# A layer with local attention and a gated unit on one core: loads and copies of the first tiles re-ordered, the last tile cut into 512 and 128 columns

## The chip, the cores and the metric

The kernel runs on one core of one Trainium2 chip. A core has five engines that run side by side, each with its own stream of instructions in program order: TensorE (PE, matrix products into PSUM; its weight loads are listed apart as PEld), VectorE (DVE), ScalarE (ACT), GpSimd (POOL) and SyncE (SP, which mainly issues DMAs). ScalarE and GpSimd can issue DMAs too; "ACTq", "POOLq" and "SPq" are the queues on which an engine issues. The metric is the device time of one execution in microseconds.

## What is computed

One layer on 2048 tokens of 640 features, in bfloat16. The input is normalised without learned weights; from it a dilated local attention and a gated unit are computed, and both are added to the input:

```python
x = A_x                                   # [1, 2048, 640]
xn = (x - mean) / sqrt(var + 1e-5)
q, k, v = split(xn @ wqkv)                # 32 heads of 20 features
idx = pos[:, None] - 2 * arange(8)        # 8 keys: this token and every second one before it
logits = einsum("bhsd,bhswd->bhsw", q, k[idx]) * 20 ** -0.5   # idx < 0: -1e9
o = einsum("bhsw,bhswd->bhsd", softmax(logits), v[idx]) @ wo
h = (xn @ w_gate) * (xn @ w_up)           # 640 -> 1536
out = x + o + h @ w_down
```

## The kernel before, in words

The 2048 tokens are 16 tiles of 128; four tiles make a chunk of 512. For each tile the input is loaded (`load_x`), VectorE computes statistics in two halves of 320 columns (`st_in`, line 251) and their aggregate (`aggr_in`, lines 257 and 259), GpSimd raises the variance to the power -0.5 (line 265), and VectorE normalises in place (`apply_in`, line 270). The normalised tile is then transposed into `xnT`. For tiles 0 to 3 TensorE does this with five transposing matmuls (line 345) in two pieces of three and two, which are copied out of PSUM piece by piece (line 351); later tiles are transposed by DMA on SP (line 339).

From `xnT` come, chunk by chunk, queries and keys with 512 columns per matmul (`qk`, lines 407 and 414), values with 320 columns (`vproj`, lines 440 and 446), and the gated unit (`glu`, lines 614, 619 and 630: gate and up products on TensorE, both copied out by ScalarE, multiplied into `hT` by VectorE). Values go out to a DRAM buffer and come back as eight shifted copies (`load_v8`). The attention of a chunk (`prodlog`, `softmax`, `av`) is VectorE's: eight products q*k (line 478, tile `pw`) whose sums over the features of a head TensorE forms in two groups of 20 matmuls (line 488, tile `pl`; one group for four of the products). ScalarE copies the logits out (line 501), SP transposes them by DMA (line 509), and then follow the softmax and the weighted sum of the values, whose result `o` SP transposes into `oT` (line 597). At the end of a chunk, `down` forms for each tile two halves of 320 output columns: 12 matmuls over `hT` and `wd` (line 652) and five over `oT` and `wo` (line 655) each; VectorE adds the residual while it takes the result out of PSUM (line 661), and a DMA stores the tile (line 683; the last two tiles are stored from SP, the others from GpSimd).

The order on each engine is made by a planner when the program is built. Every piece of work is a `Step` with an engine, a cost, the time `occ` for which it holds its engine, and dependencies. `Plan.order` simulates all engines with these numbers and emits the steps in the order of their simulated starts; of the steps that are ready it takes the one with the least time to spare to the end. So the `cost` and `floor` numbers in the code move instructions about but are no times of the chip. `load(at, fn)` makes a DMA on SP, each behind the one before it, whose data the planner counts as landed not before `at`. `inline` chains the steps of the first tiles on VectorE in the written order. `hold(wq)` is a memset of two elements of `wq`: the load of `wq` writes the same tile and so waits for it, and the place of the memset on VectorE sets when SP can issue that load. The input tiles share five buffers, so x5 waits for the last reader of x0 (the transposes of tile 0), x6 for that of x1, and so on. Results in PSUM share six banks; `pe_main` chains the matmul steps on TensorE.

In the written order of the first tiles, SP issues x0 to x3, `wq` (behind the memset, which stands after the statistics of x0), x4, `wk`, x5, x6, x7; ScalarE issues the two halves of `wv`, then loads its activation table (line 177), and issues x8 later. TensorE first multiplies zeros (line 242), then follow the transposes of tile 0, the first half of its values, the transposes of tile 1, and so on. The first piece of tile 0's transposes is copied out by ScalarE and the second by VectorE; of the other tiles ScalarE copies both.

Of the kernel before, what the change touches and what calls it, by code (L numbers as in the profile page):

```python
# [9 lines left out]
ACT = mybir.ActivationFunctionType  # L10
ALU = mybir.AluOpType
# [20 lines left out]
class Plan:  # L32
# [8 lines left out]
    def add(self, eng, cost, fn, deps=(), occ=None, after=(), kb=0):  # L41
        s = Step(eng, cost, fn, deps, occ, after)
        s.kb = kb
        s.idx = len(self.steps)
        self.steps.append(s)
        return s
# [51 lines left out]
def kernel(  # L98
# [11 lines left out]
    nc = tc.nc  # L110
    P = nc.NUM_PARTITIONS
    x_flat = A_x.flatten_outer_dims()
    out_flat = out.flatten_outer_dims()
    S, D = x_flat.shape
# [8 lines left out]
    KT = D // P  # L123
    FT = F // P
    NT = S // P
# [4 lines left out]
    NS = D // 2  # L130
# [23 lines left out]
    add = plan.add  # L154
    T = {}
# [7 lines left out]
    def load_x(t, eng=None):  # L163
        def fn():
            x = new(("x", t), [P, D], BF, "x", 5)
            (eng or nc.sync).dma_start(out=x[:], in_=x_flat[t * P : (t + 1) * P, :])
        return fn
# [3 lines left out]
    def wload(dst, src, eng=None):  # L171
        return lambda: (eng or nc.sync).dma_start(out=dst[:], in_=src.rearrange("(i p) f -> p i f", p=P))
# [9 lines left out]
    def load(at, fn, deps=()):  # L182
        s = chain[0] = add("SP", 2.0, fn, deps, occ=0.45, after=[chain[0]])
        s.floor = at
        return s
# [5 lines left out]
    def hold(dst):  # L191
        return lambda: nc.vector.memset(dst[0:1, 0, 0:2], 0.0)
# [1 line left out]
    X[0] = load(3.0, load_x(0))  # L194
    X[1] = load(3.8, load_x(1))
    X[2] = load(4.9, load_x(2))
    X[3] = load(5.3, load_x(3))

    def consts0():
        wz = new("wz", [P, CS], BF, "gs", 3)  # L200
# [32 lines left out]
    C0 = add("POOL", 0.6, consts0)  # L233
    WV = [add("ACT", 4.6, part(0), [C0], occ=0.45)]
    WV.append(add("ACT", 5.6, part(1), occ=0.45, after=[WV[0]]))
    TB = add("ACT", 1.6, table, after=[WV[1]])
    CZ = add("POOL", 3.0, consts_z, [C0], occ=1.2)

    def warm():
# [28 lines left out]
    def ln_apply(t, lo=0, hi=D):  # L268
        def fn():
            nc.vector.tensor_scalar(T["x", t][:, lo:hi], T["x", t][:, lo:hi], scalar1=T["mv", t][:, 0:1],  # L270
                                    scalar2=T["rstd", t][:], op0=ALU.subtract, op1=ALU.mult)
        return fn
# [11 lines left out]
    def inline(eng, cost, fn, deps=(), occ=None):  # L284
        s = line[eng] = add(eng, cost, fn, deps, occ=occ, after=[line.get(eng)])
        return s

    def st_in(t, g, d=None):
        return inline("DVE", 0.48, ln_stats(t, g), [d or X[t]], 0.395)
# [5 lines left out]
    def apply_in(t):  # L295
        XT[t] = inline("DVE", 0.443, ln_apply(t), [RS[t]], 0.4)
# [12 lines left out]
    def pe_main(cost, fn, deps=(), banks=1):  # L309
        nonlocal main  # L310
        waits = []
        for k in range(banks):
            if len(ring) + k >= 6:
                waits.append(ring[len(ring) + k - 6])
        main = add("PE", cost + 0.165, fn, [main, *waits, *deps], occ=cost)
        return main
# [4 lines left out]
    def transposes(t):  # L321
        c, q = divmod(t, CH)

        def slot():
            if q == 0:
                new(("xnT", c), [P, KT, CS], BF, "xnT", 2)

        def pe():
            ps = new(("pst", t), [P, KT, P], BF, "ps", 6, psum)
            for g in range(KT):  # L330
                nc.tensor.transpose(ps[:, g, :], T["x", t][:, g * P : (g + 1) * P], ident[:])

        def ev():
            slot()
            nc.scalar.copy(T["xnT", c][:, :, q * P : (q + 1) * P], T["pst", t][:])

        def dma():
            slot()
            nc.sync.dma_start_transpose(out=T["xnT", c][:, :, q * P : (q + 1) * P], in_=T["x", t][:])

        def half(g0, g1, n):
            def pe():
                ps = new(("pst", t, n), [P, KT, P], BF, "ps", 6, psum)
                for g in range(g0, g1):
                    nc.tensor.transpose(ps[:, g, :], T["x", t][:, g * P : (g + 1) * P], ident[:])  # L345

            def ev():
                if n == 0:
                    slot()
                o, i = T["xnT", c][:, g0:g1, q * P : (q + 1) * P], T["pst", t, n][:, g0:g1, :]  # L350
                nc.scalar.copy(o, i) if t or n == 0 else nc.vector.tensor_copy(o, i)  # L351
            return pe, ev

        if t < CH:
            pa, ea = half(0, 3, 0)
            pb, eb = half(3, KT, 1)
            a = pe_main(0.17, pa, [XT.get((t, 0), XT[t])])
            TX[t] = add("ACT", 0.5, ea, [a], occ=0.42)
            ring.append(TX[t])
            a = pe_main(0.11, pb, [XT[t]])  # L360
            if t:
                TT[t] = add("ACT", 0.42, eb, [a, TX[t]], occ=0.33)
                behind(VE[t - 1][0], TT[t])
            else:
                TT[t] = inline("DVE", 0.4, eb, [a], 0.33)
            ring.append(TT[t])
        elif t < XDMA:
            a = pe_main(0.28, pe, [XT[t]])
            TT[t] = add("ACT", 0.695, ev, [a], occ=0.6)
            ring.append(TT[t])  # L370
        else:
            if c == 1:
                a = TT[t] = chain[0] = add("SP", 3.0, dma, [XT[t]], occ=1.28, after=[chain[0]])
            else:
                a = TT[t] = add("SP", 2.8, dma, [XT[t], GP.get(c - 2)], occ=1.28, kb=200)
        if t + 5 < W:
            X[t + 5] = load(11.9 + 0.45 * t, load_x(t + 5), [a])
        elif t == 3:
            X[t + 5] = add("ACT", 6.0, load_x(t + 5, nc.scalar), [a], occ=0.45)
        elif 8 <= t < NT - 5:  # L380
            X[t + 5] = add("POOL", 6.0, load_x(t + 5, nc.gpsimd), [a], occ=0.45, kb=160)
# [260 lines left out]
    def down(t):  # L642
        c, q = divmod(t, CH)
        load_xr(t)
        evs = []
        def pe(n, f0, f1, wo_part):
            if f0 == 0:
                new(("psD", t, n), [P, 512], F32, "ps", 6, psum)
            ps = T["psD", t, n]
            sl = slice(n * NS, (n + 1) * NS)  # L650
            for f in range(f0, f1):
                nc.tensor.matmul(ps[:, 0:NS], lhsT=T["hT", c, f][:, q * P : (q + 1) * P], rhs=wd[:, f, sl],  # L652
                                 start=(f == 0), stop=(f == FT - 1 and not wo_part))
            for g in range(KT if wo_part else 0):
                nc.tensor.matmul(ps[:, 0:NS], lhsT=T["oT", t][:, g, :], rhs=wo[:, g, sl],  # L655
                                 start=False, stop=(g == KT - 1 and f1 == FT))

        def evict(n, a):
            def ev():
                sl = slice(n * NS, (n + 1) * NS)  # L660
                nc.vector.tensor_tensor(T["xr", t][:, sl], T["psD", t, n][:, 0:NS], T["xr", t][:, sl], ALU.add)  # L661
            e = add("DVE", 0.486, ev, [a, XR[t]], occ=0.4)
            ring.append(e)
            evs.append(e)

        hs = [HT[c, f] for f in range(FT)]
        W2 = [OE[t], WL["d"], WL["o"]]
        if q == 0:
            cut = FT - 2
            for n in range(2):  # L670
                pe_main((cut + KT) * 0.136, lambda n=n: pe(n, 0, cut, True), [*hs[:cut], *W2], banks=n + 1)
            ends = [pe_main(2 * 0.136, lambda n=n: pe(n, cut, FT, False), hs[cut:], banks=0) for n in range(2)]
            for n in range(2):
                evict(n, ends[n])
            a = ends[1]
        else:
            for n in range(2):
                a = pe_main((FT + KT) * 0.136, lambda n=n: pe(n, 0, FT, True), [*hs, *W2])
                evict(n, a)
        DT[t] = a  # L680

        def st():
            (nc.sync if t >= NT - 2 else nc.gpsimd).dma_start(out=out_flat[t * P : (t + 1) * P, :], in_=T["xr", t][:])  # L683

        OB[t] = add("SP" if t >= NT - 2 else "POOL", 2.3, st, evs, occ=0.5)


    a = st_in(0, 0)
    a = st_in(0, 1, a)
    HQ = inline("DVE", 0.08, hold(wq))  # L690
    aggr_in(0, a)
    WQ = load(8.8, wload(wq, A_wqkv[:, 0:D]), [HQ])
    X[4] = load(9.2, load_x(4))
    WK = load(11.4, wload(wk, A_wqkv[:, D : 2 * D]))
    a = st_in(1, 0)
    a = st_in(1, 1, a)
    XT[0, 0] = inline("DVE", 0.31, ln_apply(0, 0, 3 * P), [RS[0]], 0.25)
    XT[0, 1] = inline("DVE", 0.26, ln_apply(0, 3 * P, D), [RS[0]], 0.2)
    XT[0] = XT[0, 1]
# [2 lines left out]
    transposes(0)  # L702
    vproj(0, (0,))
    a = st_in(2, 0)
    apply_in(1)
    transposes(1)
    a = st_in(2, 1, a)
    aggr_in(2, a)
    vproj(0, (1,))
    vproj(1, (0,))  # L710
# [90 lines left out]
```

## Time and profile before

| | us |
|---|---|
| median of 3 runs (266.08 to 266.64) | 266.16 |
| the profiled execution | 266.25 |
| its span in the trace | 264.5 |
| TensorE busy | 258.5 |
| VectorE busy | 215.5 |
| ScalarE busy | 106.5 |
| GpSimd busy | 40.7 |

All times of the profile are from one execution and count from the start of its span; the execution itself is 1.75 us longer than the span. A row gives the start, the length, the engine, the source line, the operation, and the tile written and the tile read; "x5" means that five instructions are put together, and in square brackets stands how long the engine had been idle and what ended that. A matmul's row is longer than its share of TensorE's time, since matmuls overlap: of the matmuls with 512 columns each row has 0.379 us, but 48 of them take 10.52 us in the chain of waits. For DMA issues, the time is that on the issuing engine, and "us to landing" counts from there.

### The profile page before, as it was taken

Reading aid. Unit: us, or ns where it says so; the run is one execution under the profiler, and the core shown is the slowest. Engines: PE = TensorE matmul, PEld = TensorE weight load, DVE = VectorE, ACT = ScalarE, POOL = GpSimd, SP = SyncE. Lnnn points to the kernel's source line nnn. Section 1 sums busy time; section 2 is a strip of 40 time slices with the busy share of each in tenths; the row PEclk is TensorE's granted clock in tenths of the full one; section 3 lists DMA queues with packets and bytes.
Section 4 is the critical chain, followed back from the end, with each engine's and each line's share of the span. In section 5 each row is a group of like instructions: output and inputs, shape, how many; then the busy total and the mean of one; then the engine's idle time right before and its main releaser. Section 6 shows DMA issues by size and latency. Waiting matters only on the chain.

```text
span 264.5 us, 4077 instructions
## 1 busy us (share of the span) xinstructions
PE 258.5 (98%) x1556; PEld 140.8 (53%) x1574; DVE 215.5 (81%) x338; ACT 106.5 (40%) x196; POOL 40.7 (15%) x84
## 2 busy tenths in 40 slices
PE   7999999999999999999999999999999999999994
PEld 2645445444676546444466754644447764445773
DVE  5785998999999999999994799999938999951221
ACT  2655556655300166555510135555552005554000
POOL 4541027000021221400001000410000104000000
PEclk9999999999999999999999999999999999999999
DMA  7968996999994194983142767891109467110001
GB/s 222 372 131 244 401 341 173 369 289 255 351 239 108 35 318 146 264 290 90 25 99 72 243 223 126 235 312 25 22 15 304 151 185 214 25 25 0 27 25 50
DMA packets 50563, 46.55 MB, mean 176 GB/s; under 512 B 24642, under 2 KB 47696, under 8 KB 50544
## 3 DMA queue, kind: packets, MB, share of 16 engines
q1 hardware_dynamic: 46704, 37.26, 49.7%
q0 software_dynamic: 2384, 8.05, 8.7%
q10 hardware_dynamic: 1456, 0.98, 1.2%
q8 instruction: 12, 0.20, 0.3%
q14 instruction: 7, 0.06, 0.1%
HBM read 35.39 MB, written 5.26 MB: 154 GB/s over the span
## 4 chain that ended last, share of the span: by engine, by line
PE 97%; DVE 1%; issue 0%
PE ps L614 39%; PE ps L652 20%; PE ps L407 16%; PE ps L655 8%; PE ps L440 7%; PE pl L488 4%; PE ps L242 2%; DVE st L251 1%; PE ps L345 1%; DVE x L270 0%; DVE xr L661 0%; DVE xnT L351 0%; DVE gs L201 0%; DVE mv L257 0%; DVE ve L259 0%
## 5 line engine op out<-in xcount | busy, mean ns | idle before, releaser
L614 PE MATMUL ps<-xnT,wg 128*128 128x512 bf16 x227 | 59.0, 379 | 0.7
L614 PE MATMUL ps<-xnT,wu 128*128 128x512 bf16 x240 | 59.6, 379 | 0.0
L652 PE MATMUL ps<-wd,hT 128*128 128x320 bf16 x384 | 57.4, 299 | 0.0
L478 DVE TENSOR_TENSOR pw<-q,k 128x2560 bf16<-128x2560 bf16 x32 | 46.4, 1484 | 3.2 <-ACT k L414 2.4
L652 PEld LDWEIGHTS <-hT 128*128 128x128 bf16 x384 | 37.3, 98 | 16.3 <-issue 1.3
L575 DVE TENSOR_TENSOR v<-v,a 128x5120 bf16<-128x5120 bf16 x16 | 45.1, 2818 | 0.0
L619 ACT CAST gs<-ps 128x512 bf16<-128x512 f32 x48 | 28.1, 586 | 37.6 <-PE ps L614 37.6
L614 PEld LDWEIGHTS <-wu 128*128 128x128 bf16 x240 | 23.5, 98 | 28.3
L614 PEld LDWEIGHTS <-wg 128*128 128x128 bf16 x240 | 23.3, 98 | 28.1 <-issue 0.8
L619 ACT CAST us<-ps 128x512 bf16<-128x512 f32 x48 | 28.1, 586 | 23.3 <-PE ps L614 23.3
L661 DVE TENSOR_TENSOR xr<-ps,xr 128x320 bf16<-128x320 f32 x32 | 14.9, 484 | 19.0 <-PE ps L655 15.7
L630 DVE TENSOR_TENSOR hT<-gs,us 128x512 bf16<-128x512 bf16 x48 | 19.6, 419 | 12.6 <-ACT us L619 12.5
L683 POOL DMA_DIRECT2D out_dram<-xr x14 | 7.6, 545 | 129.2 <-DVE xr L661 129.2
L655 PE MATMUL ps<-wo,oT 128*128 128x320 bf16 x160 | 27.0, 299 | 0.0
L584 DVE TENSOR_TENSOR v<-v 128x2560 bf16<-128x2560 bf16 x16 | 23.8, 1485 | 0.1
L440 PE MATMUL ps<-wv,xnT 128*128 128x320 bf16 x160 | 23.2, 299 | 0.4 <-ACT xnT L351 0.4
L407 PE MATMUL ps<-xnT,wk 128*128 128x512 bf16 x99 | 22.4, 379 | 0.1
L407 PE MATMUL ps<-xnT,wq 128*128 128x512 bf16 x96 | 22.0, 379 | 0.2
L440 PEld LDWEIGHTS <-xnT 128*128 128x128 bf16 x160 | 15.3, 98 | 7.5 <-ACT xnT L351 0.6
L655 PEld LDWEIGHTS <-oT 128*128 128x128 bf16 x160 | 15.7, 98 | 6.1
L501 ACT CAST L<-pl 128x512 bf16<-128x512 f32 x8 | 4.7, 586 | 34.2 <-PE pl L488 32.0
L414 ACT CAST q<-ps 128x512 bf16<-128x512 f32 x20 | 11.7, 586 | 13.0 <-PE ps L407 13.0
(55 smaller groups left out, 188.9 us busy)
## 6 DMA issues: line engine op xcount, KB each, us to landing
v<-vD SPq DMA_DIRECT2D x16, 1280.0 KB, 7.5
vD<-v_t POOLq DMA_DIRECT2D x16, 160.0 KB, 3.1
xr<-in_A_x_dram POOLq DMA_DIRECT2D x16, 160.0 KB, 6.0
out_dram<-xr POOLq DMA_DIRECT2D x14, 160.0 KB, 2.2
x<-in_A_x_dram SPq DMA_DIRECT2D x12, 160.0 KB, 5.8
wg<-in_B_w_gate_dram SPq DMA_DIRECT2D x1, 1920.0 KB, 7.8
wu<-in_B_w_up_dram SPq DMA_DIRECT2D x1, 1920.0 KB, 12.0
wd<-in_B_w_down_dram SPq DMA_DIRECT2D x1, 1920.0 KB, 15.0
```

The lines of the kernel that those rows point to most:

```text
L407: nc.tensor.matmul(T[key][:, 0:n], lhsT=(wk if r else wq)[:, i, j * P : (j + 1) * P], rhs=T["xnT", c][:, i, lo : lo + n], start=(i == 0), ...
L414: nc.scalar.copy(dst, T[key][:, 0:n])
L440: nc.tensor.matmul(T["psv", t, n][:, 0:NS], lhsT=T["xnT", c][:, i, q * P : (q + 1) * P], rhs=wv[:, i, n * NS : (n + 1) * NS], start=(i == ...
L478: nc.vector.tensor_tensor(p[:], T["q", c][:], T["k", c][:, :, DIL * i : DIL * i + CS], ALU.mult)
L575: nc.vector.tensor_tensor(v[:].rearrange("p w (j h) -> p w j h", j=Dh, h=H), v[:].rearrange("p w (j h) -> p w j h", j=Dh, h=H), T["a", n][ ...
L584: nc.vector.tensor_tensor(v[:, 0:4, :], v[:, 0:4, :], v[:, 4:8, :], ALU.add)
L614: nc.tensor.matmul(ps[:], lhsT=(wu if r else wg)[:, i, f * P : (f + 1) * P], rhs=T["xnT", c][:, i, :], start=(i == 0), stop=(i == KT - 1))
L619: nc.scalar.copy(s[:], T[key][:])
L630: nc.vector.tensor_tensor(h[:], T["gs", c, f][:], T["us", c, f][:], ALU.mult)
L652: nc.tensor.matmul(ps[:, 0:NS], lhsT=T["hT", c, f][:, q * P : (q + 1) * P], rhs=wd[:, f, sl], start=(f == 0), stop=(f == FT - 1 and not wo ...
L655: nc.tensor.matmul(ps[:, 0:NS], lhsT=T["oT", t][:, g, :], rhs=wo[:, g, sl], start=False, stop=(g == KT - 1 and f1 == FT))
L661: nc.vector.tensor_tensor(T["xr", t][:, sl], T["psD", t, n][:, 0:NS], T["xr", t][:, sl], ALU.add)
```

## The change

The diff has five parts.

1. x3 is loaded on ScalarE's queue behind the two halves of `wv`, in place of SP's.
2. The memset on which the load of `wq` waits stands behind the statistics of x1 (before: behind those of x0). In the written order `wk` follows after x4, x5 and x6.
3. ScalarE copies both pieces of tile 0's transposes.
4. The statistics of x2 are both written ahead of the normalisation of tile 1, and the planner's landing times for wq, x4 to x7 and wk are other numbers.
5. The last tile's output is computed as 512 and 128 columns in place of two times 320, and each piece is stored by its own DMA.

```diff
-    X[3] = load(5.3, load_x(3))
...
+    X[3] = add("ACT", 5.0, load_x(3, nc.scalar), occ=0.45, after=[WV[1]])
-    TB = add("ACT", 1.6, table, after=[WV[1]])
+    TB = add("ACT", 1.6, table, after=[X[3]])
...
-                nc.scalar.copy(o, i) if t or n == 0 else nc.vector.tensor_copy(o, i)
+                nc.scalar.copy(o, i)
...
+            TT[t] = add("ACT", 0.42, eb, [a, TX[t]], occ=0.33)
             if t:
-                TT[t] = add("ACT", 0.42, eb, [a, TX[t]], occ=0.33)
                 behind(VE[t - 1][0], TT[t])
-            else:
-                TT[t] = inline("DVE", 0.4, eb, [a], 0.33)
...
-            X[t + 5] = load(11.9 + 0.45 * t, load_x(t + 5), [a])
+            X[t + 5] = load((11.0, 11.5, 14.2)[t], load_x(t + 5), [a])
...
+        last = t == NT - 1
+        at = [0, 512, D] if last else [0, NS, D]
...
-            sl = slice(n * NS, (n + 1) * NS)
+            sl = slice(at[n], at[n + 1])
+            ps = T["psD", t, n][:, 0 : at[n + 1] - at[n]]
...
+        if last:
+            for n in range(2):
+                add("SP", 2.1, lambda n=n: st(at[n], at[n + 1]), [evs[n]], occ=0.5)
+        else:
+            OB[t] = add("SP" if t >= NT - 2 else "POOL", 2.3, st, evs, occ=0.5)
...
     a = st_in(0, 1, a)
-    HQ = inline("DVE", 0.08, hold(wq))
     aggr_in(0, a)
-    WQ = load(8.8, wload(wq, A_wqkv[:, 0:D]), [HQ])
-    X[4] = load(9.2, load_x(4))
-    WK = load(11.4, wload(wk, A_wqkv[:, D : 2 * D]))
     a = st_in(1, 0)
     a = st_in(1, 1, a)
+    HQ = inline("DVE", 0.08, hold(wq))
+    WQ = load(10.1, wload(wq, A_wqkv[:, 0:D]), [HQ])
+    X[4] = load(10.6, load_x(4))
...
     a = st_in(2, 0)
+    a = st_in(2, 1, a)
     apply_in(1)
     transposes(1)
-    a = st_in(2, 1, a)
+    WK = load(13.6, wload(wk, A_wqkv[:, D : 2 * D]))
     aggr_in(2, a)
```

In the built program the planner's order differs in one further stretch. In chunk 1, VectorE does the fourth product q*k right behind the third, before the softmax of chunk 0; TensorE does the first group of chunk 1's logits behind the third group of chunk 0's gated unit; ScalarE's copy of these logits and SP's transposing DMA move along with it.

More of the change, by code (lines that the diff above doesn't have):

```diff
@@ L648, in pe @@
                 new(("psD", t, n), [P, 512], F32, "ps", 6, psum)
-            ps = T["psD", t, n]
-            sl = slice(n * NS, (n + 1) * NS)
+            sl = slice(at[n], at[n + 1])
+            ps = T["psD", t, n][:, 0 : at[n + 1] - at[n]]
             for f in range(f0, f1):
-                nc.tensor.matmul(ps[:, 0:NS], lhsT=T["hT", c, f][:, q * P : (q + 1) * P], rhs=wd[:, f, sl],
+                nc.tensor.matmul(ps, lhsT=T["hT", c, f][:, q * P : (q + 1) * P], rhs=wd[:, f, sl],
                                  start=(f == 0), stop=(f == FT - 1 and not wo_part))
             for g in range(KT if wo_part else 0):
-                nc.tensor.matmul(ps[:, 0:NS], lhsT=T["oT", t][:, g, :], rhs=wo[:, g, sl],
+                nc.tensor.matmul(ps, lhsT=T["oT", t][:, g, :], rhs=wo[:, g, sl],
                                  start=False, stop=(g == KT - 1 and f1 == FT))
@@ L659, in ev @@
             def ev():
-                sl = slice(n * NS, (n + 1) * NS)
-                nc.vector.tensor_tensor(T["xr", t][:, sl], T["psD", t, n][:, 0:NS], T["xr", t][:, sl], ALU.add)
-            e = add("DVE", 0.486, ev, [a, XR[t]], occ=0.4)
+                w = at[n + 1] - at[n]
+                sl = slice(at[n], at[n + 1])
+                nc.vector.tensor_tensor(T["xr", t][:, sl], T["psD", t, n][:, 0:w], T["xr", t][:, sl], ALU.add)
+            cost = 0.153 + (at[n + 1] - at[n]) / 960
+            e = add("DVE", cost, ev, [a, XR[t]], occ=cost - 0.08)
             ring.append(e)
@@ L677, in down, with st @@
             for n in range(2):
-                a = pe_main((FT + KT) * 0.136, lambda n=n: pe(n, 0, FT, True), [*hs, *W2])
+                a = pe_main((FT + KT) * ((at[n + 1] - at[n]) / 2400 + 0.003), lambda n=n: pe(n, 0, FT, True), [*hs, *W2])
                 evict(n, a)
         DT[t] = a
-        def st():
-            (nc.sync if t >= NT - 2 else nc.gpsimd).dma_start(out=out_flat[t * P : (t + 1) * P, :], in_=T["xr", t][:])
-        OB[t] = add("SP" if t >= NT - 2 else "POOL", 2.3, st, evs, occ=0.5)
+        def st(lo=0, hi=D):
+            e = nc.sync if t >= NT - 2 else nc.gpsimd
+            e.dma_start(out=out_flat[t * P : (t + 1) * P, lo:hi], in_=T["xr", t][:, lo:hi])
+        if last:
[3 more added lines that the diff above has]
+            OB[t] = add("SP" if t >= NT - 2 else "POOL", 2.3, st, evs, occ=0.5)
     a = st_in(0, 0)
     a = st_in(0, 1, a)
-    HQ = inline("DVE", 0.08, hold(wq))
     aggr_in(0, a)
-    WQ = load(8.8, wload(wq, A_wqkv[:, 0:D]), [HQ])
-    X[4] = load(9.2, load_x(4))
-    WK = load(11.4, wload(wk, A_wqkv[:, D : 2 * D]))
     a = st_in(1, 0)
     a = st_in(1, 1, a)
+    HQ = inline("DVE", 0.08, hold(wq))
+    WQ = load(10.1, wload(wq, A_wqkv[:, 0:D]), [HQ])
+    X[4] = load(10.6, load_x(4))
     XT[0, 0] = inline("DVE", 0.31, ln_apply(0, 0, 3 * P), [RS[0]], 0.25)
```

## The prediction

> **What bounds the kernel now.** First the page: TensorE is busy for 98% of the span, its granted clock reads 9 in all 40 slices, and 97% of the chain that ended last lies on it.
> ```profile
> span 264.5 us, 4077 instructions
> PE 258.5 (98%) x1556; PEld 140.8 (53%) x1574; DVE 215.5 (81%) x338; ACT 106.5 (40%) x196; POOL 40.7 (15%) x84
> ...
> PE 97%; DVE 1%; issue 0%
> ```
> Then the busy time by stretch. From 12.12 us on TensorE lacks under 1 us in 245; before that it waits. So time can come only from the head (until the first query matmul at 12.12), from the tail after the last matmul, and from the few stalls between.
> ```profile
> 5.70:12.12 6.42, 6.01 (x52) 4.01 (x52) 5.28 (x19) 3.90 (x11) 3.19 (x7) 1.00 1.07 376
> 12.12:257.00 244.88, 243.93 (x1469) 132.60 (x1485) 206.40 (x304) 101.13 (x184) 34.95 (x68) 1.00 0.60 174
> ```
> The last two columns are the DMA share and GB/s: in the head all 16 DMA engines are full (1.07). Third, the timeline of the head. The reader is to see VectorE's copy of tile 0 (6.44) ahead of the statistics of x2 (6.65) and the normalisation of tile 1 (7.05), and TensorE's waits for VectorE at 7.53 and 9.51.
> ```profile
> 4.17 0.39 SPq L172 DMA_DIRECT2D wq<-in_A_wqkv_dram  x1
> ...
> 6.44 0.29 DVE L351 COPY xnT<-ps 128x256 bf16<-128x256 bf16 x1 [0.25 <-PE ps L345]
> 6.65 0.48 DVE L251 BATCH_NORM_STATS2 st<-x 128x6 f32<-128x320 bf16 x1
> ...
> 7.05 0.43 DVE L270 TENSOR_SCALAR x<-x,mv,rstd 128x640 bf16<-128x640 bf16 x1
> ...
> 7.53 0.28 PEld L345 LDWEIGHTS <-x 128*128 128x128 bf16 x5 [0.26 <-DVE x L270]
> ...
> 7.93 1.53 PE L440 MATMUL ps<-wv,xnT 128*128 128x320 bf16 x10
> ...
> 9.02 0.43 DVE L270 TENSOR_SCALAR x<-x,mv,rstd 128x640 bf16<-128x640 bf16 x1
> ...
> 9.51 0.28 PEld L345 LDWEIGHTS <-x 128*128 128x128 bf16 x5 [0.38 <-DVE x L270]
> ```
> Fourth, the DMA view one issue at a time, last column us from issue to landing: x2 (issued 1.74), the second half of wv (1.76), x3 (2.21), wq (4.17), wk (5.18). They land at 6.44, 7.86, 7.2, 10.2 and 12.9.
> ```profile
> x<-in_A_x_dram SPq DMA_DIRECT2D x1, 160.0 KB, 4.7
> ...
> wv<-in_A_wqkv_dram ACTq DMA_DIRECT2D x1, 400.0 KB, 6.1
> ...
> x<-in_A_x_dram SPq DMA_DIRECT2D x1, 160.0 KB, 5.0
> ...
> wq<-in_A_wqkv_dram SPq DMA_DIRECT2D x1, 800.0 KB, 6.0
> ...
> wk<-in_A_wqkv_dram SPq DMA_DIRECT2D x1, 800.0 KB, 7.7
> ```
> Last, two places further on: the logits of chunk 1, and the end.
> ```profile
> 79.30 1.48 DVE L478 TENSOR_TENSOR pw<-q,k 128x2560 bf16<-128x2560 bf16 x1
> ...
> 80.63 1.45 PE L488 MATMUL pl<-pw,Ek 128*32 128x512 bf16 x20
> ```
> ```profile
> 260.33 0.84 PE L655 MATMUL ps<-wo,oT 128*128 128x320 bf16 x5
> 261.21 0.49 DVE L661 TENSOR_TENSOR xr<-ps,xr 128x320 bf16<-128x320 f32 x1 [1.82 <-PE ps L655]
> ```
> The fourth matmul of the logits needs the product that ends at 80.78, after the group has begun; other such groups of 20 take 1.19 in the chain, this one 1.38.
>
> **The change, part by part.**
> *Tile 0's copies.* The 0.29 us copy leaves VectorE; ScalarE does it in 0.38 (its 128x256 row) behind its first copy (6.23 to 6.71), so until about 7.0. The fourth matmul of the values, which needs it, stands at 6.76 + 3 x 0.136 = 7.17: free, with 0.1 us of cover. On VectorE the statistics of x2 could now start at 6.1, after the 0.15 us operation at 6.04. But x2 lands at 6.44. So I put them at 6.46 and 6.86, and the normalisation of tile 1 behind both (it stood between them) at 7.26, 0.21 later than 7.05. Transposes of tile 1 then start at 7.74, five of them take 0.28 (a chain row), ten matmuls 1.36, so tile 2's transposes could start at 9.38 instead of 9.51. VectorE is ready by then: aggregate at 7.61, statistics of x3 at 7.92 and 8.32, normalisation of tile 2 at 8.72, done 9.15. Gain 0.13. If x2 comes by 6.1, tile 1 stays at 7.53, the gap before 7.93 closes too (7.53 + 0.28 + 1.36 = 9.17) and the gain is 0.34. I take 0.13, since x2 keeps its place in its queue. From 9.51 to 12.12 TensorE has no gap, so the head passes the gain on, unless a load is late.
>
> *x3.* On ScalarE's queue it follows both halves of wv; issued at about 2.3, it costs ScalarE 0.35 (the row of x8). The table load (1.28) and the dummy activation (0.20) then end at about 4.3, and ScalarE's first copy is at 6.23: free. In the old order wv ended at 7.86 while wq already ran beside it. By the bytes per us, 1.6 MB had moved by 7.0, and wv with x0 to x3 is 1.48 MB, so without wq x3 should land at 7.0 to 7.5. Upper end: 7.86 plus 0.4 for its own 160 KB at the 376 GB/s of the stretch, 8.3. Its statistics stand at 7.92 on VectorE, and behind them in order the normalisation of tile 2: free to about 8.1. At 8.3 the normalisation ends at 9.53 and the head loses 0.05 instead of gaining.
>
> *wq, x4, x5, x6, wk.* The 0.06 us memset that frees wq moves behind the statistics of x1; VectorE's next operation at 5.27 was set by those and stays. SP issues wq at 5.3, 1.1 later. With the 6.0 us of its row it lands at 11.3; by bytes (2.3 MB are through by 9) at 9 to 10. It is wanted at 12.0: free, cover 0.7 at worst. x4 is issued right behind; x5 and x6 wait on SP for the transposes of tiles 0 and 1, as they did, and wk now waits behind x6 (8.0), so it is issued at 8.4. At 7.7 us it lands at 16.1; it is first used at 17.5. x7, behind wk, could come at 16.5 at worst, its statistics stand at 16.35; the query and key stage wants tile 7 only at 24.3. x5 no longer comes at 13.3 behind wk, so VectorE's 1.22 us wait there goes; nothing on TensorE hung on it.
>
> *What the planner makes of it.* The order of instructions moves in one place that the diff does not show. VectorE does the fourth product of chunk 1 at once after the third, not at 79.30, and TensorE does those 20 logit matmuls after three groups of the gated unit. In the old times TensorE reaches them at 46.33; the product starts at 44.58 and ends at 46.06, so they do not wait, with 0.27 to spare. The stall at 80.63 (1.38 - 1.19 = 0.19) goes. VectorE runs 1.4 later through chunk 0, but so does TensorE (1.19): the h tile that ends at 69.0 is read at 70.2, cover 1.0. The extra ScalarE copy (0.59) and the transposing DMA moved on SP ahead of that of output tile 0 lie in idle time (ScalarE is 40% busy). Ends: +0.19 and, if the product is late as at 80.63, 0.
>
> *Last tile.* 34 matmuls of 320 at 0.136 are 4.62. Now 17 of 512 at 10.52/48 = 0.219 are 3.73 and 17 of 128 at the transposes' 0.28/5 = 0.056 (same shape, with their weight loads) 0.95: 4.68, 0.06 longer. The first eviction (about 0.69) is hidden under the 0.95. The last one shrinks: 0.168 for 14 columns and 0.484 for 320 give 0.29 for 128, 0.20 less. The last store moves 32 KB instead of 160; of its 1.8 us to landing some 0.55 is movement. Between nothing saved and nearly all of it, I take 0.2, as packets of 256 B appear in no plain store here. The extra issue on SP (0.35) is done before the last eviction. Gain 0.20 - 0.06 + 0.2 = 0.34; ends 0.14 and 0.6.
> [...]
>
> **Sum.** 0.13 + 0.19 + 0.34 = 0.66. The profiled execution took 266.25 (span 264.5 and 1.75 around it), so 265.6; the median of three is 0.09 lower: 265.5.
>
> **The rivals.**
> *Slack without profit:* x2 or x3 gates the head and the store's fixed part holds the tail: gain 0 + 0.19 + 0.14 = 0.33, 265.8. The landing of x2 at 6.44, just before 6.65, speaks for it.
> *Narrow matmuls paced by weight loads:* a load's own mean is 98 ns, not 56. So paced the 17 take 1.67, the last tile 3.73 + 1.67 = 5.40, which is 0.78 longer, and the tail gives 0.20 + 0.2 - 0.78 = -0.38; with 0.13 and 0.19 the sum is -0.06: 266.2. Against it: five transposes, with as many loads, in 0.28.
> [...]
> *Slower:* x3 is starved behind wv. Past 8.1 us each us of x3 is a us at 9.51, since normalisation 2 stands behind its statistics on VectorE. With wk's 7.7 us it would land at 10.0: loss 1.8, against 0.53 gained elsewhere, 267.4. It decides from a landing at 8.8; slower by 0.2% from 9.3. For it: ScalarE's second half took 6.1. Against: after 7.1 that queue was empty while SP's moved 0.38 MB per us.
>
> **How the numbers follow.** A measurement of this kernel tells about 0.2%, 0.53 us, from no change. Forecast 0.58; the two rivals without profit 0.15 and 0.12; slower 0.12; the last 0.03 is for a stall not thought of. Nine tenths of the forecast's own range (265.1 to 265.7) lie below 265.63, so faster 0.52; the rest of it and the two rivals make same 0.33; slower 0.15. The range reaches from 265.0 (0.34 + 0.19 + 0.6 gained) to 266.5, into the slower case.
>
> **What would show it.** Right: the first query matmul at 11.8 to 12.0; x3's statistics without a DMA wait; the logits of chunk 1 near 46 with 1.19; the last landing about 0.3 us sooner after the last matmul. [...]

## The result and the profile after

The changed kernel takes 265.2 us (median of 8 runs, 265.02 to 265.85) against 266.12 (8 runs beside it, 265.97 to 266.64). The ratio is 0.9967, with a 95% interval of 0.9955 to 0.9979: faster by 0.92 us, and even the near end of the interval (0.21%) is just beyond the 0.2% that a measurement of this kernel can tell. The forecast was 265.5 and faster. The profiled execution took 265.12, its span is 263.4, so the time around the span stays (1.72 against 1.75) and the gain is all in the span.

The page of the changed kernel, its first lines:

```profile
span 263.4 us, 4099 instructions
...
PE 258.4 (98%) x1574; PEld 139.6 (53%) x1574; DVE 215.5 (82%) x337; ACT 106.7 (41%) x197; POOL 40.7 (15%) x84
```

TensorE's busy time reads the same (258.4 against 258.5), and the span is 1.1 us shorter. The busy time by stretch, with the same bounds as before (length, then PE, PEld, DVE, ACT, POOL, granted clock, DMA share, GB/s):

```profile
5.70:12.12 6.42, 5.95 (x52) 4.02 (x53) 4.98 (x18) 4.56 (x14) 3.54 (x11) 1.00 1.05 356
12.12:257.00 244.88, 244.88 (x1485) 132.21 (x1484) 206.71 (x305) 100.66 (x183) 34.60 (x64) 1.00 0.62 175
```

The middle stretch now has no gap that the records show, where 0.95 us was lacking before. Most of that is no time gained: the two kernels do the same matmuls, but the trace before has 18 records fewer (1556 against 1574, 16 of them in this stretch), and a missing record reads as a gap. A second trace of the changed kernel, with 1555 records, reads 244.28 us busy of the 245.28 from its first query matmul to 257. To see where the 1.1 us went, take the same instruction in both traces and subtract the starts. The timeline of the head after the change:

```profile
6.00 0.75 ACT L351 COPY xnT<-ps 128x384 bf16<-128x384 bf16 x2 [1.59 <-PE ps L345]
6.20 0.89 DVE L251 BATCH_NORM_STATS2 st<-x 128x6 f32<-128x320 bf16 x2
...
7.00 0.43 DVE L270 TENSOR_SCALAR x<-x,mv,rstd 128x640 bf16<-128x640 bf16 x1
...
7.48 0.28 PEld L345 LDWEIGHTS <-x 128*128 128x128 bf16 x5 [0.43 <-DVE x L270]
...
7.75 0.89 DVE L251 BATCH_NORM_STATS2 st<-x 128x6 f32<-128x320 bf16 x2
7.78 1.52 PE L438 MATMUL ps<-wv,xnT 128*128 128x320 bf16 x10
...
9.04 0.36 PEld L345 LDWEIGHTS <-x 128*128 128x128 bf16 x5
...
11.73 5.56 PE L405 MATMUL ps<-xnT,wq 128*128 128x512 bf16 x25
```

VectorE's copy is gone (ScalarE does two, 6.00), x2's statistics start at 6.20 instead of 6.65, and everything behind follows: tile 1's transposes still wait for VectorE (0.43) and start at 7.48 instead of 7.53, tile 2's at 9.04 wait for nothing, and the first query matmul starts at 11.73 instead of 12.12. In the chain that ended last, x2's load now stands in front of the statistics:

```profile
1.73 4.44 DMA x<-in_A_x_dram
6.20 0.89 DVE st L251 x2
7.49 0.45 PE ps L345 x5
...
46.10 1.19 PE pl L486 x20
```

The last of these rows is the group of chunk 1's logits that was at 80.70 with 1.38. On VectorE its product ends at 41.38 + 4.29 = 45.67, before TensorE comes to it:

```profile
41.38 4.29 DVE L476 TENSOR_TENSOR pw<-q,k 128x2560 bf16<-128x2560 bf16 x3
```

And the end of the timeline, then the two stores in the view of DMA issues (KB, us from issue to landing):

```profile
255.82 2.75 PE L653 MATMUL ps<-wd,hT 128*128 128x512 bf16 x12
...
258.41 1.24 PE L656 MATMUL ps<-wo,oT 128*128 128x512 bf16 x5
...
259.49 0.83 PE L653 MATMUL ps<-wd,hT 128*128 128x128 bf16 x12
259.69 0.69 DVE L663 TENSOR_TENSOR xr<-ps,xr 128x512 bf16<-128x512 f32 x1 [3.18 <-PE ps L656]
...
260.16 0.44 PE L656 MATMUL ps<-wo,oT 128*128 128x128 bf16 x5
260.64 0.29 DVE L663 TENSOR_TENSOR xr<-ps,xr 128x128 bf16<-128x128 f32 x1 [0.26 <-PE ps L656]
```

```profile
out_dram<-xr SPq DMA_DIRECT2D x1, 128.0 KB, 1.7
out_dram<-xr SPq DMA_DIRECT2D x1, 32.0 KB, 1.5
```

| place | before | after | gained so far | of it here |
|---|---|---|---|---|
| first query matmul | 12.12 | 11.73 | 0.39 | 0.39 |
| queries of chunk 2 | 90.23 | 89.66 | 0.57 | 0.18 |
| last eviction starts | 261.21 | 260.64 | 0.57 | 0 |
| last eviction ends | 261.70 | 260.93 | 0.77 | 0.20 |
| end of span | 264.5 | 263.4 | 1.1 | 0.3 |

### The profile page after: what moved, and what is told of

Same layout as the page of the kernel before. It is cut to its first block, busy times and chain, and to the rows that moved or that the text cites. A ratio compares the mean times of both kernels' runs of the same rounds, so it can differ in the third digit from the quotient of the medians.

```text
span 263.4 us, 4099 instructions
## 1 busy us (share of the span) xinstructions
PE 258.4 (98%) x1574; PEld 139.6 (53%) x1574; DVE 215.5 (82%) x337; ACT 106.7 (41%) x197; POOL 40.7 (15%) x84
## 4 chain that ended last, share of the span: by engine, by line
PE 96%; DMA 2%; DVE 1%; SPq 0%; issue 0%
PE ps L612 39%; PE ps L653 20%; PE ps L405 16%; PE ps L656 8%; PE ps L438 8%; PE pl L486 4%; DMA x<-in_A_x_dram 2%; PE ps L345 0%; DVE st L251 0%; SPq L166 0%; DVE x L270 0%; DVE xr L663 0%
## 5 line engine op out<-in xcount | busy, mean ns | idle before, releaser
L612 PE MATMUL ps<-xnT,wg 128*128 128x512 bf16 x240 | 59.7, 379 | 0.0
L653 PE MATMUL ps<-wd,hT 128*128 128x320 bf16 (+2 forms) x384 | 57.4, 299 | 0.0
L663 DVE TENSOR_TENSOR xr<-ps,xr 128x320 bf16<-128x320 f32 (+2 forms) x32 | 14.9, 483 | 18.8 <-PE ps L656 15.5
L656 PE MATMUL ps<-wo,oT 128*128 128x320 bf16 (+2 forms) x160 | 27.0, 299 | 0.0
```

Of the source, the lines that this page charges most:

```text
L612: nc.tensor.matmul(ps[:], lhsT=(wu if r else wg)[:, i, f * P : (f + 1) * P], rhs=T["xnT", c][:, i, :], start=(i == 0), stop=(i == KT - 1))
L653: nc.tensor.matmul(ps, lhsT=T["hT", c, f][:, q * P : (q + 1) * P], rhs=wd[:, f, sl], start=(f == 0), stop=(f == FT - 1 and not wo_part))
L656: nc.tensor.matmul(ps, lhsT=T["oT", t][:, g, :], rhs=wo[:, g, sl], start=False, stop=(g == KT - 1 and f1 == FT))
```

## The experiments

The trace leaves three things open. Is the larger gain of the head (0.39 where 0.13 was forecast) due to the loads that were moved, or to x2 landing earlier by itself? Which of the five parts carry the gain? And how near was the load of x3 to costing time? Theory A: x3's packets, on SP's queue in front of or beside the others, held up x2, so that moving x3 paid in the head. Theory B: `wq`'s later start let x2 land sooner. The rival: x2's landing scatters by itself, and only the copy matters. A third theory: `wq`'s data, if it starts early, makes x3 late. Unless said otherwise one execution was taken per kernel; the kernel before took 266.03 beside the first four, 266.21 beside the next four, and 266.19 (median of 8) beside the last four.

**x3 back on SP's queue** (the changed kernel otherwise).

```diff
     X[2] = load(4.9, load_x(2))
+    X[3] = load(5.3, load_x(3))
...
-    X[3] = add("ACT", 5.0, load_x(3, nc.scalar), occ=0.45, after=[WV[1]])
-    TB = add("ACT", 1.6, table, after=[X[3]])
+    TB = add("ACT", 1.6, table, after=[WV[1]])
```

> The changed kernel with x3 back on SP's queue, fourth behind x0 to x2. In the changed kernel x2 landed at 6.13 instead of 6.44 and the first query matmul came at 11.73 instead of 12.12. Theory A: x2 came sooner because x3's packets left its queue. Then x2 lands at 6.4 here, the statistics of x2 start at 6.46, tile 1 is normalised 0.25 later than in the changed kernel, and the first query matmul is at 11.95 to 12.0. Theory B: x2 came sooner because wq's transfer starts 1.1 us later. Then x2 stays at 6.1 and the first query matmul at 11.7 to 11.75. In both x3 lands by 7.2 and is not waited for.

Measured: 264.95, the first query matmul at 11.59, x2 landed at 5.4, earlier than in the changed kernel. Theory A falls: with x3 on SP x2 is not late. The 6.1 of theory B was not met either.

**The memset of wq back behind the statistics of x0.**

```diff
     a = st_in(0, 1, a)
+    HQ = inline("DVE", 0.08, hold(wq))
     aggr_in(0, a)
+    WQ = load(10.1, wload(wq, A_wqkv[:, 0:D]), [HQ])
+    X[4] = load(10.6, load_x(4))
     a = st_in(1, 0)
     a = st_in(1, 1, a)
-    HQ = inline("DVE", 0.08, hold(wq))
-    WQ = load(10.1, wload(wq, A_wqkv[:, 0:D]), [HQ])
-    X[4] = load(10.6, load_x(4))
```

> The changed kernel with the memset that frees wq back behind the statistics of x0, so that SP issues wq at 4.2. Theory A (x2 gained from x3's leaving its queue): x2 stays at 6.1. Theory B (x2 gained from wq's later start): x2 lands at 6.4. A third theory, that holding wq serves x3: x3 stands behind wv on the other queue, and wq's 800 KB beside it move its landing from 7.73 to 8.2 or later; its statistics then hold the normalisation of tile 2, whose transposes move from 9.13 to 9.4 or later, and the first query matmul to 12.0 or later. If neither load is touched, the first query matmul stays at 11.73 or is 0.06 later for the memset on VectorE.

Measured: 265.25, first query at 11.90. Not x3 but x2 was late here, and the timeline shows the wait:

```profile
6.36 0.89 DVE L251 BATCH_NORM_STATS2 st<-x 128x6 f32<-128x320 bf16 x2 [0.19 <-DMA x<-in_A_x_dram]
```

Taken alone this would blame the early `wq`. But x2 landed at 5.5 to 5.7 in three other kernels with the early `wq` (table below), and at 6.3 in one with the late `wq`, so theory B is not borne out. The third theory falls: x3's statistics start at 7.82 without a wait.

**VectorE copies tile 0's second piece again**, and the second half of x2's statistics stands behind tile 1's normalisation.

```diff
-                nc.scalar.copy(o, i)
+                nc.scalar.copy(o, i) if t or n == 0 else nc.vector.tensor_copy(o, i)
...
-            TT[t] = add("ACT", 0.42, eb, [a, TX[t]], occ=0.33)
             if t:
+                TT[t] = add("ACT", 0.42, eb, [a, TX[t]], occ=0.33)
                 behind(VE[t - 1][0], TT[t])
+            else:
+                TT[t] = inline("DVE", 0.4, eb, [a], 0.33)
...
     a = st_in(2, 0)
-    a = st_in(2, 1, a)
     apply_in(1)
     transposes(1)
+    a = st_in(2, 1, a)
```

> The changed kernel with the second piece of tile 0's transposes copied by VectorE again, in the old place ahead of the statistics of x2; the loads stay as changed. The planner then also puts the fourth product of chunk 1 and its logits back to their old place near 80. Theory: the copy holds VectorE in the head, so tile 2's transposes return to about 9.45 and the first query matmul to 12.05 (0.3 later), and the 20 logit matmuls near 80 take 1.38 instead of 1.20 again; in all 0.5 us longer than the changed kernel, span 263.9. Rival: the head's gain is that of the loads; then the first query matmul stays at 11.73 and only the 0.18 at the logits return.

Measured: 265.62, first query at 12.06. In the chain the logits are back at their old place, with their old length:

```profile
80.65 1.38 PE pl L488 x20
```

So the copy and the order of x2's statistics together carry the head's gain (0.33 against the changed kernel), and the planner's early product comes along with them (0.19). Together that is 0.52; the run is 0.50 longer than the changed kernel's profiled execution. No run separates the copy from that order; the run with the early product, below, bears on it.

**wk ahead of x5 and x6.**

```diff
     X[4] = load(10.6, load_x(4))
+    WK = load(11.4, wload(wk, A_wqkv[:, D : 2 * D]))
...
-    WK = load(13.6, wload(wk, A_wqkv[:, D : 2 * D]))
```

> The changed kernel with wk ahead of x5 and x6 on SP's queue again. Theory of the prediction: nothing on TensorE hangs on it; x5 comes later than 10.9 and VectorE waits for it, but the query and key stage of chunk 1 starts as before: the span stays within 0.05 of 263.4. Rival: wk beside wq takes bandwidth from wq, so that the first query matmul waits for wq; then it is later than 11.73 and the span by as much.

Measured: 265.03, first query at 11.65. VectorE waits 0.60 for x4 (0.52 in the changed kernel) and then 1.43 for x5, TensorE for nothing: the order is worth nothing, as costed.

**The last tile's cut alone, on the kernel before** (all other lines as they were; the edit is part 5 of the change).

```diff
+        last = t == NT - 1
+        at = [0, 512, D] if last else [0, NS, D]
...
+        if last:
+            for n in range(2):
+                add("SP", 2.1, lambda n=n: st(at[n], at[n + 1]), [evs[n]], occ=0.5)
```

> The kernel before with the last tile's cut and its two stores alone. From the changed kernel's trace: matmuls of the last tile as long as before (3.67 for the 512 columns and 0.95 for the 128, against 4.62), last eviction 0.29 instead of 0.49, landing 1.5 us after issue instead of 1.8: 0.50 in all, span 264.0; the first query matmul stays at 12.1. Rival, the prediction's own terms: 0.34, span 264.15. If the narrow matmuls were paced by their weight loads elsewhere than in the changed kernel, the tail would gain nothing.

Measured: 265.62, 0.59 below the kernel before beside it, span 263.9 against 264.5. Its first query (12.10) and last eviction (261.18, before 261.21) stand where they did, so the gain is behind the last matmul: 0.20 of the eviction and the rest in the store, 32 KB landing in 1.4.

**The cut, but one store of 160 KB for the last tile** (the changed kernel otherwise).

```diff
-        if last:
-            for n in range(2):
-                add("SP", 2.1, lambda n=n: st(at[n], at[n + 1]), [evs[n]], occ=0.5)
-        else:
-            OB[t] = add("SP" if t >= NT - 2 else "POOL", 2.3, st, evs, occ=0.5)
+        OB[t] = add("SP" if t >= NT - 2 else "POOL", 2.3, st, evs, occ=0.5)
```

> The changed kernel with the last tile still cut into 512 and 128 columns but stored whole (160 KB) behind the second eviction. Theory: the store of 32 KB is what landed 0.3 sooner, so the landing is again 1.8 us after issue and the span 0.3 longer, 263.7. Rival: a store's time to landing does not hang on its size here and 1.5 was the scatter of one execution; then the span stays at 263.4.

Measured: 265.36, span 263.7, though its head was 0.13 earlier than the changed kernel's (11.60). The last eviction ends at 260.80 and the span 2.9 later, where it is 2.5 in the changed kernel. The store in its view:

```profile
out_dram<-xr SPq DMA_DIRECT2D x1, 160.0 KB, 1.8
```

So the small last store is worth 0.3 by its landing and 0.4 by the span, whose end is given to 0.1.

**The early product alone, on the kernel before.** The planner is told to take the products of chunk 1 as soon as they are ready; loads, copies and tail stay.

```diff
+            if c == 1 and g == 0:
+                for j in (1, 2, 3):
+                    PW[8 + j].urgent = True
             LASTPW[c] = PW[m]
```

> The kernel before with the fourth product of chunk 1 done right behind the third, so that the planner puts the 20 logit matmuls behind the third group of the gated unit as in the changed kernel; loads, copies and the last tile as before. Theory: the logits take 1.20 there instead of 1.38 near 80, and the gain stays to the end: span 264.3 (0.18 shorter), the first query matmul of chunk 0 at 12.1. Rival: VectorE's 1.4 us later in chunk 0 brings a new wait at the output of the chunk, which takes the 0.18 back.

Measured: 265.93, and the logits in the chain:

```profile
46.32 1.19 PE pl L491 x20
```

From the first query matmul to the queries of chunk 2 it takes 89.88 - 11.95 = 77.93 against 90.23 - 12.12 = 78.11: 0.18, and no later wait. The rest of its 0.28 is the head (11.95): tile 0's transposes took 0.54 here and 0.72 in the trace before, and VectorE's copy, which waits for them, started at 6.26 instead of 6.44.

This run also shows what the copy can do without the new order of x2's statistics. Between the two halves of these stands the normalisation of tile 1, which needs GpSimd's result:

```profile
6.27 0.55 POOL L265 TENSOR_TENSOR rstd<-ve,mhalf 128x1 f32<-128x1 f32 x1 [1.06 <-DVE ve L259]
...
6.87 0.43 DVE L270 TENSOR_SCALAR x<-x,mv,rstd 128x640 bf16<-128x640 bf16 x1
```

The result is there at 6.82, so even with no copy on VectorE this normalisation could come only 0.05 sooner, and in the old order the second half of the statistics stays behind it. So an estimate for the copy alone, from these rows, is a first query near 11.9 to 11.95. In the run with `wk` ahead, tile 1 is normalised no sooner (6.92), but both halves of the statistics stand ahead of it, and the first query is at 11.65. By this estimate a good part of what the copy brings comes of the order, which puts work of VectorE into its wait for GpSimd.

**x3 behind x4 on ScalarE's queue.**

```diff
-    X[3] = add("ACT", 5.0, load_x(3, nc.scalar), occ=0.45, after=[WV[1]])
+    X[4] = add("ACT", 5.0, load_x(4, nc.scalar), occ=0.45, after=[WV[1]])
+    X[3] = add("ACT", 5.0, load_x(3, nc.scalar), occ=0.45, after=[X[4]])
...
-    X[4] = load(10.6, load_x(4))
```

> The changed kernel with x4 on ScalarE's queue between wv and x3, so that x3 lands later by one load of 160 KB: about 8.1 to 8.2 instead of 7.73. Theory of the prediction's slower case (x3's statistics stand ahead of the normalisation of tile 2 on VectorE, free until about 8.1, then one us per us): statistics at 8.2, normalisation of tile 2 at 9.0, its transposes at 9.45 to 9.5 instead of 9.13, the first query matmul 0.3 to 0.4 later, 12.05 to 12.1. Rival: the queues share the engines so that x3 comes no later; then 11.7 as in the changed kernel.

Measured: 264.93, first query at 11.56. x3 was not later for 160 KB more in front of it: its statistics start at 7.61, in the changed kernel at 7.75. The expected delay did not come, and the run says nothing on the price of a late x3; the last run below does.

**The copy and the tail alone, on the kernel before**: no load is moved. Five executions.

```diff
-                nc.scalar.copy(o, i) if t or n == 0 else nc.vector.tensor_copy(o, i)
+                nc.scalar.copy(o, i)
...
+            TT[t] = add("ACT", 0.42, eb, [a, TX[t]], occ=0.33)
             if t:
-                TT[t] = add("ACT", 0.42, eb, [a, TX[t]], occ=0.33)
                 behind(VE[t - 1][0], TT[t])
-            else:
-                TT[t] = inline("DVE", 0.4, eb, [a], 0.33)
...
+        last = t == NT - 1
+        at = [0, 512, D] if last else [0, NS, D]
...
     a = st_in(2, 0)
+    a = st_in(2, 1, a)
     apply_in(1)
     transposes(1)
-    a = st_in(2, 1, a)
```

> The kernel before with two parts of the change only: ScalarE copies all of tile 0 (with both statistics of x2 ahead of the normalisation of tile 1, and the early product that the planner makes of it), and the last tile's cut. All loads stay as before: x3 on SP's queue, wq's memset behind the statistics of x0, wk ahead of x5 and x6. Theory now: the copy, the product and the tail are the whole gain; the first query matmul at 11.6 to 11.75 where x2 lands by 6.1, span 263.3 to 263.5, time 0.9 to 1.1 below the kernel before and within 0.2 of the changed kernel. Rival: issuing wq early costs something (11.90 was seen once with it); then the first query matmul is at 11.9 and the time 0.2 to 0.3 above the changed kernel.

Measured: 264.94 (264.90 to 265.26), ratio to before 0.9952 (0.9938 to 0.9966). That is 1.25 below the kernel before, more than the 0.9 to 1.1 expected. The one trace, of its longest execution (265.26), has the first query at 11.91 and not at 11.6 to 11.75, though x2 landed at 5.5; the last section comes back to it.

**The changed kernel again, beside it.** Five executions.

> The changed kernel once more, on the same chip as the two beside it: 0.9 to 1.0 below the kernel before. x2 has landed between 5.4 and 6.4 in the executions so far; by the waits seen, the first query matmul is at 11.6 when it lands by 6.0 and up to 0.3 later when it lands at 6.4.

Measured: 264.99 (264.94 to 265.43), ratio 0.9957 (0.9944 to 0.9970). It is 1.20 below the kernel before, where 0.9 to 1.0 was expected and 0.92 was measured first; why the same two kernels lie 0.28 further apart here stays open. The two intervals, each some 0.7 us wide, lie nearly on each other: the load moves of parts 1, 2 and 4 are worth nothing that can be measured, and the copy with the order of x2's statistics (and the early product that the planner makes of them) and the tail are the whole gain.

**x3 on SP's queue, timed**: the kernel of the first experiment. Five executions.

> The changed kernel with x3 on SP's queue, fourth behind x0 to x2, as in the first set, now timed. Theory: x3's queue is worth nothing; same time as the changed kernel within 0.15. Rival: the 264.95 of the one execution was a real gain of 0.15 or more.

Measured: 265.21 (264.93 to 265.57), ratio 0.9961 (0.9948 to 0.9974). The median is 0.22 above the changed kernel's, more than the 0.15 expected, but the intervals overlap widely: no gain by SP's queue is seen, and no loss is shown. In the profiled execution x2 landed at 6.3 and its statistics waited 0.23 for it; in the first experiment the same program had x2 at 5.4. That is the scatter itself, shown with one program.

**x3 on SP's queue behind wq**: the slower rival made true.

```diff
-    X[3] = add("ACT", 5.0, load_x(3, nc.scalar), occ=0.45, after=[WV[1]])
-    TB = add("ACT", 1.6, table, after=[X[3]])
+    TB = add("ACT", 1.6, table, after=[WV[1]])
...
-    WQ = load(10.1, wload(wq, A_wqkv[:, 0:D]), [HQ])
+    WQ = load(0.0, wload(wq, A_wqkv[:, 0:D]), [HQ])
+    X[3] = load(0.0, load_x(3))
     X[4] = load(10.6, load_x(4))
```

> The changed kernel with x3 on SP's queue behind wq, issued at about 5.7, so that it lands late for certain: by the bytes ahead of it between 9 and 10.5. Theory of the slower case: its statistics start at the landing, the normalisation of tile 2 0.8 behind, tile 2's transposes 1.3 behind, instead of at 9.0 to 9.1; the first query matmul comes 1.3 to 2.7 later than 11.65, by the landing plus 1.3 minus 9.05, and the span grows by as much. Rival: wq and the later work have slack that takes up part of it; then less.

Measured: 269.88, span 268.2. Its timeline, and three stretches of it:

```profile
11.26 0.89 DVE L250 BATCH_NORM_STATS2 st<-x 128x6 f32<-128x320 bf16 x2 [3.17 <-DMA x<-in_A_x_dram]
...
12.55 0.71 PE L344 MATMUL ps<-ident,x 128*128 128x128 bf16 x5 [2.90 <-DVE x L269]
...
13.05 2.68 PE L437 MATMUL ps<-wv,xnT 128*128 128x320 bf16 x10
```

```profile
9.00:12.50 3.50, 0.65 (x5) 0.24 (x3) 1.24 (x4) 0.63 (x2) 0.00 (x0) 0.93 1.07 373
12.50:16.50 4.00, 3.95 (x25) 2.74 (x26) 3.02 (x11) 2.07 (x6) 3.11 (x14) 0.64 0.46 153
12.05:15.40 3.35, 2.85 (x14) 1.87 (x15) 2.58 (x10) 1.51 (x4) 2.28 (x8) 0.50 0.69 230
```

x3 lands at 11.24, later than the 9 to 10.5 expected; by the expectation's own sum (landing plus 1.3 minus 9.05) the first query would be 3.49 later than 11.65, at 15.14. It is at 16.53. By the rival's price (9.51 + 11.24 - 8.1) tile 2's transposes start at 12.65; they start at 12.55. But the first query comes 16.53 - 12.55 = 3.98 behind them instead of 11.73 - 9.13 = 2.60 in the changed kernel. The additional 1.38 is not waiting: in that stretch TensorE is busy throughout, and its granted clock is 0.64, the last column but two. In finer stretches it is 1.00 from 11.00 to 11.90, 0.50 from 12.05 to 15.40 and 1.00 from 15.45 to 16.50. Ten value matmuls take 2.68 in their row instead of 1.52. TensorE stood still from 9.65 to 12.55, for 2.90 us, and the clock fell between 11.90 and 12.05, 2.25 to 2.40 us after its last matmul. What sets that moment, and the end of the slow stretch, this one run does not show.

## Why the prediction came out as it did

*Head: forecast 0.13, measured 0.39 in the pair of traces.* The step's structure held, and its input did not. The first query at 11.73 lies just outside the 11.8 to 12.0 that was named as a sign of being right. Set the starts of x2's statistics, the landing of x2 and the first query matmul side by side (us; landings by issue and duration, to 0.1):

| kernel | tile 0's second copy | wq issued | x2 landed | x2's statistics | first query | difference |
|---|---|---|---|---|---|---|
| before | VectorE | early | 6.4 | 6.65 | 12.12 | 5.47 |
| its tail cut | VectorE | early | 5.6 | 6.62 | 12.10 | 5.48 |
| its product early | VectorE | early | 5.7 | 6.47 | 11.95 | 5.48 |
| copy back on VectorE | VectorE | late | 6.2 | 6.59 | 12.06 | 5.47 |
| changed | ScalarE | late | 6.2 | 6.20 | 11.73 | 5.53 |
| changed, again | ScalarE | late | 5.7 | 6.15 | 11.72 | 5.57 |
| wk ahead | ScalarE | late | 5.6 | 6.13 | 11.65 | 5.52 |
| one store | ScalarE | late | 5.9 | 6.08 | 11.60 | 5.52 |
| x3 on SP | ScalarE | late | 5.4 | 6.07 | 11.59 | 5.52 |
| x3 on SP, timed | ScalarE | late | 6.3 | 6.33 | 11.87 | 5.54 |
| x3 behind x4 | ScalarE | late | 5.6 | 6.03 | 11.56 | 5.53 |
| memset of wq early | ScalarE | early | 6.3 | 6.36 | 11.90 | 5.54 |
| copy and tail alone | ScalarE | early | 5.5 | 6.07 | 11.91 | 5.84 |

In the VectorE rows the second half of x2's statistics stands behind the normalisation of tile 1, in the ScalarE rows ahead of it, so the column stands for both.

The forecast put the statistics at 6.46 and the first query at 12.12 - 0.13 = 11.99, 5.53 later: just what nearly all ScalarE rows show. What failed is the sentence "But x2 lands at 6.44 ... x2 keeps its place in its queue": the landing of one execution was taken for a constant of the order, and it scatters from 5.4 to 6.5 whatever is behind it. The forecast gave 0.13 for x2 at 6.44 and 0.34 for x2 by 6.1. By the rows, with the mean of the VectorE rows at 12.06, it is 0.23 for the three ScalarE rows with x2 at 6.2 to 6.3 (mean 11.83), 0.39 for the six with x2 by 6.1 (mean 11.67), and 0.33 over all nine (11.73). With VectorE's copy in the way an early x2 was worth nothing (second row: landed 5.6, statistics at 6.62), which is why the profile before could not show it.

*x3, wq, x4 to x6, wk: forecast free.* Right, by the four runs that undo one load move each (x3 twice, `wq`, `wk`) and by the copy and tail alone. x3's landing was forecast at 7.0 to 7.5, with 8.3 as the upper end; it came at 7.7 in the changed kernel, and VectorE took it at 7.75. Its normalisation then ended at 8.99, and TensorE, without a wait in its rows, began the transposes at 9.13, so of the cover "to about 8.1" hardly 0.1 was left there: the earlier head had used it up. Nothing was lost, but it was nearer than the forecast made it.

*Early product: forecast 0.19, measured 0.18*, in the change and alone, with no new wait on the h tiles.

*Tail: forecast 0.34, measured 0.50.* The eviction's 0.20 was exact. The longer matmuls (0.06) were not there: the 512s take 259.49 - 255.82 = 3.67 for 17, 0.216 each, where 0.219 had been taken from a chain row of 48 in 10.52. That row lies in a stretch of 10.79 (12.28 to 23.07) in which the trace before lacks a record: the changed kernel's chain has 50 such matmuls in the same 10.79, which is 0.216. With 0.95 for the 128s the sum is 4.62, as before. The store was taken at 0.2, the author's estimate between nothing and 0.55, since no plain store of the kernel before had rows of 256 bytes; it was 0.3: its packets moved for 0.60 us before (262.58 to 263.18) and for 0.26 after (261.81 to 262.07), so the movement that was saved is the whole difference.

*Sum: forecast 0.66, measured 0.92 by the medians and 1.13 by the profiled executions* (266.25 to 265.12), and 1.20 by the medians of the last runs, whose 264.99 lies at the low end of the stated range (265.0). The three terms as measured one by one, 0.33, 0.18 and 0.50, make 1.01. Two terms were too small: the head's, where the lower of two worked-out ends was taken (0.13 of 0.13 and 0.34), and the store's (0.2 between 0 and 0.55, measured 0.3).

*The rivals.* Slack without profit is refuted by the two terms that came out larger. Narrow matmuls paced by weight loads is refuted: twelve start in 259.49 to 260.16, 0.056 each, where the rival took 0.098. The store's fixed part did not hold the tail either: in the DMA view, in slices of 0.11 us, the 256-byte rows of the last store moved at 150 GB/s at most and the 1,024-byte rows of the one before it at up to 355, but the last store still landed 1.5 us after its issue, against 1.8 for 160 KB. The slower rival was not met: x3 landed 1.1 us before the point from which it decides. The run with x3 behind `wq` bears out its price for the wait (12.65 by the price, 12.55 measured), but not for the whole: the slower clock behind the wait, which no term of the prediction has, cost 1.38 more.

## What to carry to other kernels

A landing time in one trace is one draw (x2: 5.4 and 6.3 in two executions of one program). Before it is made the term that limits a gain, ask what the engine's own order would give if the data came 1 us sooner, and keep both values as equals. A copy that is cheap for a busy engine's clock time can still stand at the head of a chain; here moving 0.29 us of it to an idle engine, with the statistics of x2 put into the place that it left, the early product that the planner made of this, and cutting the last piece of output small, made the whole gain, and the re-ordered loads none. And count the records of two traces before you compare their busy time: 18 missing matmuls looked like waiting here.

## What the runs showed that was not expected

- x2, third in its queue, lands between 5.4 and 6.5 us in fourteen executions (the thirteen of the table and the run with x3 behind `wq`, 6.5), and at 5.4 and 6.3 in two executions of one program. Neither x3's queue nor `wq`'s start orders these values. What sets them stays open.
- The ten matmuls on zeros at the start (512 columns) take between 3.70 and 4.45 us, and ten of 512 columns later take 2.16 (50 in 10.79). The column of the granted clock does not show this: in the trace before it reads 1.00 from 1.27 to 5.70. In the run of copy and tail alone they took 4.45, the first transposes 0.71 and the first five value matmuls 1.11 (changed kernel: 3.91, 0.54 and 0.85), and the head lost the 0.3 by which its last column differs: there TensorE, not VectorE, came last to tile 1. Four other ScalarE rows had 4.45 too and lost nothing, so the rows to read are those of the first tile. What makes these first matmuls slow, and by different amounts, no run here shows.
- Two of the first eight runs of the changed kernel lie 0.6 above the rest (265.82 and 265.85). Either of these two scatters is large enough in the head for much of it; no trace of those two runs is at hand, so this is only argued.
- In the run with x3 behind `wq`, a stop of TensorE of 2.90 us cost 1.38 us more behind it, by a granted clock of 0.50 for 3.35 us (0.64 as the mean of 4). A late load in a head can be dearer than its lateness.
